# The keys' transform of a long convolution, brought into the values' form

## The chip, the cores and the metric

The kernel runs on one core of a Trainium2 chip. The metric is the device time of one execution in microseconds (us), taken over several runs; their median is compared. A profiled execution gives a span (first to last instruction) and a trace of every instruction.

## The reference

Two results of 2048 rows by 576 columns are put side by side. The first (A) is a state-space convolution: for each of 576 channels a filter K of 2048 taps is computed from 128 complex exponentials and convolved with the input u. The second (B) is linear attention with 32 heads of 18, whose features are two softmaxes.

```
A = -exp(log_A_real) + 1j * A_imag
C = (C_real + 1j * C_imag) * dt[:, None]
P = exp((A * dt[:, None])[:, :, None] * pos[None, None, :])
K = 2.0 * einsum("dn,dnl->dl", C, P).real
Kf, Uf = rfft(K, 2 * L), rfft(u_t, 2 * L)
y = irfft(Uf * Kf, 2 * L)[:, :, :L] + u * D_skip
...
phi = concatenate([softmax(p), softmax(-p)])        # of q and of k, per head
o = (phi_q @ (phi_k.T @ v)) / (phi_q @ sum(phi_k) + 1e-6)
out = concatenate([y, o @ wo])
```

The change concerns only the two transforms of A: that of the filter (in the names of the program the keys, `kd`, `kb`, `ks`) and that of the input u (here called the values, `ud`, `ub`).

## The kernel before

**Stages.** B reads 16 key tiles of 128 rows (`key_tile`) and later 16 query tiles (`query_tile`); their matrix products (`gemm`) use pairs of weights `wh`/`wl` and `vh`/`vl`. For A, 36 groups of 16 channels (`phases`, `waves`, `sizes_of`, `group`) build the filter into the tile `ks`; each nine groups complete a quarter of the channels. The transforms of length 4096 are done in two steps with the result of the first step going through DRAM:

- `u_first` (16 calls): the input's first step, 64 rows to 128 with the weights `w1`, written to `ud`.
- `k_first` with `first` (16 calls, four for each quarter): the filter's first step, 32 rows to 64 with `w1[:, 0:64]`; the eight matmuls of a call use eight tiles of TensorE's array (32 rows by 64 columns each) at once. Two stores of 64 partitions take the result to `kd`, of which there is one for each half of the channels.
- `product` (16 calls: 8 sets of frequencies `p` for each of the 2 halves): the second step of both, their product, and the first step back. Its parts are named p1 to p4. In p1 the values: 16 matmuls of 64 by 32 with the weights `ff`, on eight tiles at once, into `pu`, copied to `us`. In p2 (`times`, twice) the keys: four matmuls of 128 by 64 with the weights `fk`, a table of its own loaded twice per product, into `pk`, and a multiply by `us` on VectorE. In p3 four sums that make complex products of real ones (GpSimd or VectorE). In p4 the way back (`back`, 32 by 64), a copy and a store to `zd`.
- `last` (16 calls): the last step back, with `w3`, and the store to the output.

**Order.** Nothing is scheduled at run time. `body` only lists 2506 operations with what each reads and writes (`op`, `Plan`); the table `ORDER` at the end of the file gives the sequence in which they are emitted. In it a number is an operation, `x` takes its second engine (VectorE for ScalarE, for instance), `@` gives the PSUM banks that it takes (eight banks, 0 to 7), and `:n` puts n matmuls on zeros ahead of it, which write nothing that counts and keep TensorE occupied (line L244 of the profile, in `emit`). `Plan.run` refuses an order in which an operation stands ahead of what it needs. Each engine, and the queue SP from which all transfers are issued, works its share of the sequence strictly in that order. Buffers come from pools of fixed numbers (`tags`): a name with 2 has two buffers in turn, and who takes the third waits for the first.

Nearly all matmuls go through the helper `mm`, so they share line L302 of the profile and are told apart by the tiles they read: `kb,fk` (keys' second step), `ub,ff` (values' second step), `ks,w` (keys' first step), `ub,w` (values' first step), `ac,ff` and `cs,ff` (way back). Copies have line L307, sums L317, multiplies L321. A row such as `128*64 128x288 f32 x256` is a weight tile of 128 rows by 64 columns over 288 columns of data; TensorE executes an f32 matmul as two instructions.

## Time and profile before

| what | value |
|---|---|
| time, three runs | 551.81 us median (550.91 to 556.78) |
| profiled execution | 553.84 us, span 552.1 us |
| TensorE busy | 534.9 us (97%) |
| VectorE / ScalarE / GpSimd busy | 458.7 / 379.3 / 325.0 us |
| moved by DMA | 111.07 MB, 201 GB/s mean |
| granted TensorE clock | 0.997 mean |

Busy time of an engine is the time in which at least one of its instructions runs. Matmuls are pipelined, so a group's mean duration is longer than the distance at which they follow each other, and the groups' busy times add up to more than the engine's. "Idle before" is the time in which the engine stood still just ahead of an instruction, with what ended it.

### The profile page before, as it was taken

The numbers are of one execution on the slowest core, as the hardware profiler recorded it, in microseconds if no ns is written. First come the engines' busy times: TensorE is split into PE (matmuls) and PEld (weight loads), VectorE is DVE, ScalarE is ACT, GpSimd is POOL, SyncE is SP. The second block draws the span as 40 slices with busy tenths as digits, with TensorE's granted clock in tenths as the row PEclk, the third lists the DMA queues.
The fourth block names the chain that finished last, engine by engine and source line by source line (L and its number), as shares of the span: only waits on it lengthen the run. The fifth ranks groups of instructions, "written<-read, shape, count | busy, mean of one in ns | idle before, by whom it ended". The sixth has DMA issues, their size and how long they took to land.

```text
span 552.1 us, 18539 instructions
## 1 busy us (share of the span) xinstructions
PE 534.9 (97%) x7812; PEld 442.8 (80%) x7812; DVE 458.7 (83%) x757; ACT 379.3 (69%) x547; POOL 325.0 (59%) x473
## 2 busy tenths in 40 slices
PE   8999799999999999999999999999999999999997
PEld 7999799899978887988887766878976765776886
DVE  7999999989777999999999999998885776767541
ACT  4788857997569999897799868968873244213422
POOL 1365856787499887974599848988144245234300
PEclk9999999999999999999999999999999999999999
DMA  8964130332746778248673798675876888898976
GB/s 224 337 201 136 68 135 26 97 98 84 247 105 191 230 247 268 75 147 244 227 239 113 215 265 263 207 245 179 271 241 153 225 267 250 285 281 266 295 245 158
DMA packets 90368, 111.07 MB, mean 201 GB/s; under 512 B 5938, under 2 KB 74546, under 8 KB 90286
## 3 DMA queue, kind: packets, MB, share of 16 engines
q1 hardware_dynamic: 90286, 109.90, 65.2%
q8 instruction: 61, 1.00, 0.8%
q14 instruction: 21, 0.17, 0.1%
HBM read 65.34 MB, written 44.54 MB: 199 GB/s over the span
## 4 chain that ended last, share of the span: by engine, by line
PE 70%; DVE 11%; DMA 8%; ACT 6%; issue 3%; SPq 0%; POOL 0%; ACTq 0%; DVEq 0%
PE psum L302 64%; PE psum L557 3%; DMA ff<-in_ff_dram 2%; DMA x<-xd 1%; PE psum L244 1%; PE psum L585 1%; DMA dram<-zo 1%; DMA out_dram<-ot 1%; DMA zo<-in_xT_dram 1%; DVE small L450 1%; DMA dram<-zi 1%; DMA pa<-in_par_dram 1%; DVE x L317 1%; DVE small L441 1%; DVE e L317 1%
## 5 line engine op out<-in xcount | busy, mean ns | idle before, releaser
L302 PE MATMUL psum<-wh,x 128*128 128x288 f32 x576 | 126.0, 305 | 5.1 <-DVE x L317 3.2
L302 PE MATMUL psum<-vh,x 128*128 128x288 f32 x576 | 123.6, 301 | 0.9 <-DVE zo L307 0.8
L765 POOL TENSOR_TENSOR cs<-cs,pi 128x128 int32<-128x128 int32 (+4 forms) x180 | 105.8, 592 | 8.2
L302 PEld LDWEIGHTS psum<-wh,x 128*128 128x128 f32 x576 | 95.2, 190 | 12.5 <-issue 4.6
L302 PEld LDWEIGHTS psum<-vh,x 128*128 128x128 f32 x576 | 94.2, 188 | 7.0 <-issue 3.1
L302 PE MATMUL psum<-wl,x 128*128 128x288 f32 x320 | 94.4, 297 | 0.0
L302 PE MATMUL psum<-vl,x 128*128 128x288 f32 x320 | 93.7, 295 | 0.0
L317 POOL TENSOR_TENSOR e<-e,small 128x576 f32<-128x576 f32 (+1 forms) x28 | 46.9, 1675 | 32.0 <-DVE small L321 21.9
L819 ACT ACTIVATE psum<-psum 128x512 f32<-128x512 f32 x108 | 58.8, 583 | 9.2 <-PE psum L302 8.5
L302 PEld LDWEIGHTS psum<-wl,x 128*128 128x128 f32 x320 | 60.8, 190 | 0.0
L302 PEld LDWEIGHTS psum<-vl,x 128*128 128x128 f32 x320 | 60.2, 188 | 0.0
L823 DVE TENSOR_TENSOR cs<-psum,cs 128x1024 f32<-128x1024 f32 x36 | 43.8, 1215 | 4.5 <-ACT psum L819 4.0
L317 POOL TENSOR_TENSOR x<-zo,x 64x128 fp32r<-64x128 f32 (+1 forms) x34 | 29.7, 873 | 29.8 <-ACT x L401 28.3
L824 DVE TENSOR_TENSOR cs<-psum,cs 128x1024 f32<-128x1024 f32 x36 | 43.7, 1213 | 2.0 <-ACT psum L819 1.8
L448 ACT ACTIVATE e<-e 128x1152 f32<-128x1152 f32 x32 | 37.3, 1166 | 11.0 <-POOL e L317 6.2
L317 POOL TENSOR_TENSOR ac<-ac 128x288 f32<-128x288 f32 x36 | 29.0, 825 | 26.7 <-DVE ac L321 22.1
L453 POOL TENSOR_TENSOR o<-e 128x576 f32<-128x576 f32 x16 | 21.1, 1319 | 38.6 <-ACT e L448 37.8
L302 PEld LDWEIGHTS psum<-kvb,fT 126*128 126x128 f32 (+1 forms) x320 | 38.5, 188 | 5.6 <-issue 2.9
L302 PE MATMUL psum<-kvb,fT 126*128 126x133 f32 (+1 forms) x320 | 41.5, 279 | 0.0
L302 PEld LDWEIGHTS psum<-cs 128*32 128x32 f32 x2304 | 34.0, 110 | 8.4 <-issue 3.3
L307 ACT ACTIVATE zi<-psum 128x576 f32<-128x576 f32 x40 | 25.0, 648 | 21.4 <-PE psum L302 14.9
L302 PE MATMUL psum<-cs 128*32 128x64 f32 x2304 | 39.5, 220 | 0.0
(154 smaller groups left out, 1161.2 us busy)
## 6 DMA issues: line engine op xcount, KB each, us to landing
dram<-zi SPq DMA_DIRECT2D x16, 576.0 KB
dram<-zi SPq DMA_DIRECT2D x32, 288.0 KB
kb<-dram SPq DMA_DIRECT2D x32, 288.0 KB
ub<-dram SPq DMA_DIRECT2D x32, 288.0 KB
dram<-zo SPq DMA_DIRECT2D x32, 288.0 KB
zo<-in_xT_dram SPq DMA_DIRECT2D x24, 320.0 KB
zi<-dram SPq DMA_DIRECT2D x12, 576.0 KB
ub<-in_u_dram SPq DMA_DIRECT2D x16, 288.0 KB
```

Source lines behind the costliest of these rows:

```text
L244: self.matmul(t[0:cols, 0:n], self.zero.t[0:rows, 0:cols], self.data.t[0:rows].bitcast(BF16)[:, 0:n], start=not o[13], stop=not o[13], ski ...
L302: pe.matmul(o, l, r, start=start, stop=stop, skip_group_check=skip)
L307: op(("act", "dve"), (c_act(n), c_dve(n)), lambda e: act.activation(dst(), src(), AF.Copy) if e == "act" else dve.tensor_copy(dst(), src() ...
L317: op(eng, [c_dve(n[0]) if e == "dve" else c_pool(n[1]) for e in eng], lambda e: (dve if e == "dve" else pool).tensor_tensor(dst(), a(), b( ...
L441: op("dve", c_dve(D), lambda: dve.tensor_reduce(two(ends.t[:, :, 0]), v(), axis=AX.X, op=ALU.max, negate=True), r=[p], w=[ends])
L448: op("act", c_act(1152) + 40, lambda: act.activation(e.t, e.t, AF.Exp), r=[e], w=[e], table="exp")
L453: op("pool", c_pool(470), lambda: pool.tensor_tensor(pair.t, e.t[:, :, :, 0:9], e.t[:, :, :, 9:18], op=ALU.add), r=[e], w=[pair], lock=True)
L557: pe.transpose(tp.t[0:m, j - j0, :], e.t[:, sign, 7 * g:7 * g + GRP[g], :].rearrange("p h f -> p (h f)"), ident.t)
L765: op("pool", c_pool(2 * n * W), lambda n=n, j=j: pool.tensor_tensor(x()[:, :, :, n:2 * n], x()[:, :, :, 0:n], pi.t[:, j:j + 2, gs].bitcast ...
L819: op("act", c_act(512), lambda b=b: act.activation(b.t, b.t, AF.Exp), r=[b], w=[b], table="exp")
L823: op("dve", c_dve(64 * W), lambda: dve.tensor_tensor(F(), both(M.t), F(), op=ALU.mult), r=[M, cs], w=[cs])
L824: op("dve", c_dve(64 * W), lambda: dve.tensor_tensor(E.t[:, :, :, 32:64], both(up.t), cs.t[:, :, :, 0:32], op=ALU.mult), r=[up, cs], w=[E])
```

## The change

The filter's transform takes the form that the input's has.

- The first step makes 128 rows of 64, as `u_first` does, where it made 64 of 32. Since `ks` holds the filter in blocks of 32 rows, the 64 rows are summed in two halves: four matmuls of 32 by 128 with one half of the new table `kf`, and four with the other half that accumulate on them. The result goes to `kd` with one store of 128 partitions.
- The second step uses `ff`, the weights of the values, in the same 16 matmuls of 64 by 32. The function `turn` holds eight of them (one of two parts) and fills one pair of PSUM banks; a product calls it twice for the values and twice for the keys. The table `fk` and its 32 loads are gone.
- The multiply takes the values' both parts and one part of the keys; a sum then needs the results of both multiplies. All these tiles are `ac` (now three buffers) or `cs`; `us2`, `kb` and `fk` no longer have buffers of their own, and `ub` has five.
- `ORDER` is a new table throughout (2475 operations); the matmuls on zeros in it number 102 where there were 122.

```diff
-    return dict(w1=f(np.concatenate([w1, np.concatenate([f1, f1]), f2], 1)), fk=f(fk), ff=f(np.concatenate([fu, fi], 2)))
+    return dict(w1=f(np.concatenate([np.concatenate([f1, f1]), f2], 1)), kf=f(np.tile(f1.reshape(32, 256), (4, 1))), ff=f(np.concatenate([fu, fi], 2)))
...
-          2: "v1 o pi mg ff ub kb zo us2 ac zi", 3: "e fk x9 ot", 5: "cs", 7: "small"})
+          2: "v1 o pi mg ff zo zi", 3: "e x9 ot ac", 5: "cs ub", 7: "small"})
...
     def k_first(qt, ks):
         def one(j):
             o = B("zi", [128, 8, 4, DQ])
-            src = lambda m, c: ks.t[32 * m:32 * m + 32, 16 * j + 8 * c:16 * j + 8 * c + 8, :].rearrange("p b d -> p (b d)")
-            first(ks, src, HD, o, lambda m: o.t[:, :, 2 * m:2 * m + 2].rearrange("p b m d -> p m b d"), lambda p: p.rearrange("p m (b d) -> p m b d", b=8))
-            for c in range(2):
...
+            ps = [B("ps", [128, 2, HD], banks=2) for _ in range(2)]
+
+            def f():
+                for r in range(2):
+                    for m in range(4):
+                        mm(ps[m // 2].t[:, m % 2], kf.t[32 * m:32 * m + 32, r], ks.t[32 * m:32 * m + 32, 32 * r + 8 * j:32 * r + 8 * j + 8, :].rearrange(
+                            "p b d -> p (b d)"), r == 0, r == 1, True)
+            op("pe", 970, f, r=[kf, ks], w=ps, mode=(32, 128))
...
+        def bring(b, z, cols):
+            for par in range(2):
+                op("sp", c_dma(128 * 2304, 1152), lambda par=par: sp.dma_start(b[par].t, four(z, par)[:, :, cols]), r=[z], w=[b[par]])
+
+        def turn(b, part):
+            po = B("ps", [128, 2, HD], banks=2)
+
+            def f():
                 for c in range(4):
                     for r in range(2):
...
+                        mm(po.t[32 * c:32 * c + 32, r], fu()[64 * r:64 * r + 64, c, part, :], b[c % 2].t[64 * r:64 * r + 64, c // 2])
+            op("pe", 490, f, r=[ff, *b], w=[po], mode=(64, 32))
+            return po
+        bring(ub, ud, cs)
+        pl.step("p1")
+        home = "cs" if half and p % 2 else "ac"
+        us = B(home, [128, 2, 2, HD])
+        for part in range(2):
+            pu = turn(ub, part)
+            copy("any", lambda part=part: us.t[:, :, part], lambda pu=pu: pu.t, [pu], [us], D)
+        pl.step("p2")
+        bring(kb, kd[half], slice(0, HD))
+        acs = []
+        for part in range(2):
+            pk, ac = turn(kb, part), B(home, [128, 2, 2, HD])
+            tt("dve", lambda ac=ac: ac.t, lambda: us.t, lambda pk=pk: pk.t[:, :, None].to_broadcast([128, 2, 2, HD]), ALU.mult, [us, pk], [ac], 4 * HD)
+            acs.append(ac)
...
-        op("pe", 970, back, r=[ff, *acs], w=pz, mode=(32, 64))
+        op("pe", 970, back, r=[ff, *done, re], w=pz, mode=(32, 64))
...
-0 1 2 1125 4 1131 1192 3 5 1132 1135 1124 1134 34 51 35@0:26 20 27 1133 1137 1136 1138 6 36 359 1024 1139 52 28@2:23 29 53 39 1156 1140 1141 1155 40
+0 1 2 4 3 5 1132 1136 1135 1124 1186 1133 34 1134 51 20 1137 35@0:26 36 39 52 21@2:10 22 37 53 1138 1139 1148 1140 1155 1141 1142 1143 1105 38 27 1144
```

In the order of the instructions a row gives line, instruction, the tile written and those read, the shape, and how many follow each other. Line L302 of before is L288 of the change. On TensorE the first product that is emitted (half 0) stood so before:

```order
L302 MATMUL psum<-vl,x_4031 128x288
L302 MATMUL psum<-cs 32x64 x32
L302 MATMUL psum<-ub,ff 32x288 x16
L302 MATMUL psum<-kb,fk 64x288 x8
L302 MATMUL psum<-sel,mg 128x512 x4
```

and stands so with the change, where `ub,ff` is written for the values and for the keys alike:

```order
L571 MATMUL psum<-ident,o 128x128 x4
L572 MATMUL psum<-ident,o 128x128
L288 MATMUL psum<-ub,ff 32x288 x8
L288 MATMUL psum<-cs 32x64 x32
L288 MATMUL psum<-ub,ff 32x288 x24
L288 MATMUL psum<-sel,mg 128x512 x2
```

The values' 16 matmuls are two calls of eight, with a group's matmuls (`cs`) between them, and the keys' 16 follow the second call at once; the 8 of `kb,fk` are gone.

Later, on TensorE, a product of the second half (number 11, counted from 0) stood so before, with the way back of another product (`cs,ff`) and query tiles (`kvb,fT` and `ident,e`) between its values and its keys:

```order
L557 MATMUL psum<-ident,e 126x128 x4
L302 MATMUL psum<-ub,ff 32x288 x16
L302 MATMUL psum<-kvb,fT 128x133 x2
L302 MATMUL psum<-kvb,fT 128x76 x2
L557 MATMUL psum<-ident,e 126x128 x4
L302 MATMUL psum<-cs,ff 64x288 x16
L302 MATMUL psum<-kb,fk 64x288 x8
```

and the same product now:

```order
L543 MATMUL psum<-ident,e 72x128 x2
L288 MATMUL psum<-ub,ff 32x288 x32
L288 MATMUL psum<-kvb,fT 128x133 x6
L288 MATMUL psum<-vh,x_6832 128x288
L288 MATMUL psum<-vl,x_6832 128x288
```

All four calls follow each other in one tiling, each into a pair of banks (in the table pairs 0, 4, 6 and again 0), and query tiles' products come behind them.

On SP's queue the loads of the first products stood so before (`zi` to DRAM is the store of a first step):

```order
L634 DMA dram<-zi 128x1152 x3
L923 DMA kb<-dram 128x2x288 x2
L898 DMA ub<-dram 128x2x288
L891 DMA ff<-in_ff_dram 128x512
L898 DMA ub<-dram 128x2x288
L921 DMA fk<-in_fk_dram 128x256 x2
```

and now:

```order
L656 DMA mg<-gd 64x768
L608 DMA dram<-zi 128x1152
L886 DMA ub<-dram 128x2x288
L877 DMA ff<-in_ff_dram 128x512
L886 DMA ub<-dram 128x2x288 x3
```

The loads of `fk` are no longer in the queue; those of the keys have the line and the name of the values' loads.

266 lines of the change are left out of this document (108 added, 158 removed).

## The prediction

> **What bounds the kernel now.** I read the page first: engines, slices, the chain of waits by engine.
>
> ```profile
> span 552.1 us, 18539 instructions
> PE 534.9 (97%) x7812; PEld 442.8 (80%) x7812; DVE 458.7 (83%) x757; ACT 379.3 (69%) x547; POOL 325.0 (59%) x473
> ...
> PE 70%; DVE 11%; DMA 8%; ACT 6%; issue 3%; SPq 0%; POOL 0%; ACTq 0%; DVEq 0%
> ```
>
> TensorE is busy for 97% of the span and carries 70% of the chain that ended last. 552.1 - 534.9 = 17.2 us are all that it stood idle. The share is an average, so next come four stretches (busy us of each engine, granted clock, DMA share, GB/s).
>
> ```profile
> 0.00:110.00 110.00, 104.94 (x1446) 96.78 (x1447) 102.46 (x161) 82.14 (x112) 60.57 (x105) 0.98 0.50 153
> 110.00:265.00 155.00, 152.59 (x2566) 132.37 (x2568) 137.33 (x242) 128.14 (x184) 116.24 (x167) 1.00 0.57 175
> 265.00:400.00 135.00, 135.00 (x2165) 104.37 (x2155) 124.33 (x196) 113.89 (x163) 100.33 (x154) 1.00 0.72 224
> 400.00:552.10 152.10, 142.33 (x1655) 109.26 (x1653) 94.57 (x161) 55.14 (x92) 47.81 (x48) 1.00 0.82 242
> ```
>
> From 110 to 400 us TensorE lacks 2.4 us of 290: work added to or taken from it there moves the end one for one. Ahead of 110 us VectorE is nearly as full. Behind 400 us TensorE idles for 152.1 - 142.3 = 9.8 us while the DMA engines are busy for 0.82 of the time: there the transfers share in the bound.
>
> What the change touches on TensorE are four groups of the view of groups by line and form (busy us, mean ns of one execution; an f32 matmul is executed twice, so 128 matmuls read x256).
>
> ```profile
> L302 PE MATMUL psum<-kb,fk 128*64 128x288 f32 x256 | 35.7, 414 | 1.4 <-DVE ac L936 0.8 <-DVE cs L321 0.4 <-DVE fT L307 0.2
> L302 PE MATMUL psum<-ub,w 64*128 64x288 f32 x128 | 20.8, 424 | 0.1
> L302 PE MATMUL psum<-ub,ff 64*32 64x288 f32 x512 | 19.5, 408 | 2.1 <-DMA ff<-in_ff_dram 2.1
> L302 PE MATMUL psum<-ks,w 32*64 32x288 f32 x256 | 13.2, 426 | 1.3 <-issue 1.3
> ```
>
> `kb,fk` is the keys' second transform, `ub,ff` the values' second one, `ks,w` the keys' first one, `ub,w` the values' first one. Busy time here is the time in which at least one matmul of the group runs, so these sums can be compared across tilings.
>
> **The keys' second transform.** Removed: 16 products times 8 matmuls of 128 rows by 64 columns, 35.7 us. Added: 16 times 16 matmuls of 64 by 32 over the same 288 columns with the same `ff` weights, which is what `ub,ff` is: 19.5 us. Change: -16.2 us. The other end: if each of the 32 new calls stood alone between other tilings, it would cost what a lone call of eight tiles costs, 0.67 us from 421.08 to 421.75 in the timeline below, 32 x 0.67 = 21.4, and the change -14.3. I take -16.2, since the new order mostly puts such calls side by side.
>
> **The keys' first transform.** Removed: 16 calls of 8 matmuls of 32 by 64, all eight tiles at once, 13.2 us. Added: 16 calls of 8 matmuls of 32 by 128, four tiles at once, two deep (the second accumulates on the first). The trace has no 32 by 128 form. Its nearest row is `ub,w`, 64 by 128, two tiles at once and two deep, 16 calls as well: 20.8 us, +7.6. Bounds: 13.2 us (nothing added) below. Above, the call has sixteen weight loads against eight in `ub,w`; could only two run at a time, a call would take twice as long, 41.6 us, +28.4. The rows of the loads speak against that end: in `ks,w` the sixteen loads of a call span 0.23 us, although four row groups are addressed.
>
> ```profile
> 28.54 1.24 PE L302 MATMUL psum<-ub,w 64*128 64x288 f32 x8
> 29.71 0.40 PE L302 MATMUL psum<-vh,x 128*128 128x288 f32 x1
> ...
> 421.08 0.74 PE L302 MATMUL psum<-ks,w 32*64 32x288 f32 x16
> 421.75 0.40 PE L302 MATMUL psum<-wh,x 128*128 128x288 f32 x1
> ...
> 421.08 0.23 PEld L302 LDWEIGHTS psum<-ks,w 32*64 32x64 f32 x16 [0.17 <-issue]
> ...
> 434.73 2.16 PE L302 MATMUL psum<-kb,fk 128*64 128x288 f32 x16 [0.16 <-DVE fT L307]
> 436.82 0.38 PE L302 MATMUL psum<-kvb,fT 126*128 126x133 f32 x1
> ```
>
> **Sum, made twice.** From the groups: -16.2 + 7.6 = -8.6 us. From single visits (start of a call to start of what follows): call one pass of all tiles that work at once a round. `kb,fk` has 16 executions on 2 tiles, 8 rounds in 2.09 us; `ks,w` 16 on 8, 2 rounds in 0.67. So a round is 1.42 / 6 = 0.237 us and a visit adds 0.20. `ub,w`, 8 on 2, should then take 4 x 0.237 + 0.20 = 1.15; it took 1.17. Rounds before: 128 + 32 + 64 (`ub,ff`) = 224. Rounds after: 64 + 64 + 64 = 192. 32 x 0.237 = 7.6 us less. Counted over the two orders, TensorE changes its tiling 240 times before and 228 times after, which at 0.20 is 2.4 us less: -10.0 in all. I take -8.6, since the groups cover all calls and not three.
>
> The page TensorEngine Tiling of the Trainium skill (Key Properties) says that a change of tiling drains TensorE; the 0.20 us of a visit agree with it. By that rule the 12 changes saved are real and the sum is -10.0; without it they are nothing and the rounds alone give -7.6.
>
> **Loads and stores.** Dropped: 32 loads of `fk` and 32 issues on SP's queue; one `kf` load comes early.
>
> ```profile
> q1 hardware_dynamic: 90286, 109.90, 65.2%
> ...
> dram<-zi SPq DMA_DIRECT2D x32, 288.0 KB
> ...
> fk<-in_fk_dram SPq DMA_DIRECT2D x32, 128.0 KB
> ...
> L921 SPq DMA_DIRECT2D fk<-in_fk_dram x32: 333/458/1183, 275.8 to 495.3; - x32
> ```
>
> 32 x 128 KB = 4.2 MB of 109.9 MB, so about 4.2 / 109.9 x 65.2% x 552 = 14 us of all DMA engines, half of it behind 400 us. SP issues them in 32 x 0.46 = 15 us, in line with the `ub`, `kb` and `zo` transfers. On the path I count 0: TensorE waited for transfers of a product only 2.1 us (`ff`, above). At best these 2.1 us go. The first transform's 32 stores become 16 of double size; the last of each half may land later by one old store, and covered it is by other products and query tiles; uncovered I bound it at 1.5 us a half.
>
> **The rest of a product.** Two copies and two multiplies of the same sizes stay, and four sums of 288 (over all products 45 of 64 on GpSimd instead of 49). One wait is new: a sum needs both multiplies instead of one.
>
> ```profile
> POOL ac L317 <- DVE ac L321: 22.1, 6, 7.1
> ```
>
> GpSimd already waits 22.1 us for these multiplies. The first sum of a product can wait one multiply longer, 1.35 us (row under the banks, below); behind it on GpSimd stand the angle steps of the kernel's groups and the query tiles' sums, which ScalarE and VectorE wait for, and TensorE's last step of the product waits for the sums. From 265 to 400 us GpSimd is idle for 34.7 of 135, so I count 0; uncovered it is at most 16 x 1.35 = 21.6 us, an end that would need GpSimd on the path, where the chain has it at 0%.
>
> The matmuls that only keep TensorE occupied (L244) go from 122 to 102. They stand where the old order expected a wait, so I count 0; at best 20 x 10.8 / 71 = 3 us.
>
> ```profile
> L244 PE MATMUL psum<-ident,zero 128*128 128x256 bf16 x71 | 10.8, 320 | 1.5 <-DVE zero L340 1.5
> ```
>
> **The new order as a whole.** Its waits can't be read from a trace of the old one. I take the 17.2 us of idle as they are. One of them shows how far they can move:
>
> ```profile
> 64.77 0.29 PE L302 MATMUL psum<-wl,x 128*128 128x288 f32 x1
> 68.23 0.61 PE L302 MATMUL psum<-wh,x 128*128 128x288 f32 x1 [3.17 <-DVE x L317]
> ...
> 68.00:71.50 3.50, 3.27 (x14) 3.27 (x15) 3.50 (x6) 2.87 (x4) 1.76 (x3) 0.54 0.49 157
> ```
>
> A wait of 3.17 us was followed by 3.5 us at a granted clock of 0.54, which loses 3.5 x 0.46 = 1.6 more: 4.8 us in one place that the change doesn't touch. A new order can lose it or have a second one. TensorE: Matmul & The Clock Gate of the Trainium skill (Part 1) puts the threshold at an idle window of about 3.4 us; this trace agrees in kind: behind 110 us, where no wait is named that is as long, the clock stands at 1.00.
>
> **Result of the sum.** The profiled execution took 553.84 us, 1.7 more than its span; 553.8 - 8.6 = 545.2. It stands 2.0 above the median of the three runs, 551.8; on that footing the forecast is 543.2, 1.6% less.
>
> **Rivals.**
> *The tail gives nothing (no change).* Eight of the sixteen products run behind 400 us. If transfers set the pace there, their share of 16.2, 8.1 us, turns into waits, and 552.1 - 0.5 = 551.6 is left (551.3 as median). For it: DMA share 0.82, 9.8 us idle. Against: 2.1 MB fewer are moved there too, about 7 us of the DMA engines' time, so both resources shrink alike. Chance 0.25.
>
> *Banks (slower).* The new calls come in runs of up to four, each into a pair of the eight PSUM banks. A run is 8 rounds, 1.9 + 0.2 us. The pairs come free only after two copies and two multiplies:
>
> ```profile
> L307 DVE COPY us<-psum 128x576 f32<-128x576 f32 x12 | 8.8, 748 | 1.9 <-PE psum L302 1.8
> L321 DVE TENSOR_TENSOR ac<-us,psum 128x1152 f32<-128x1152 f32 x24 | 31.6, 1351 | 3.7 <-PE psum L302 3.0 <-ACT zo L307 0.2
> ```
>
> 0.75 + 2 x 1.35 = 3.45 us of VectorE's time stays as it is, and TensorE, through sooner by 1.0 us a product, meets the same full banks. If it then waits 1.0 us each time, the 16.2 us are lost, the +7.6 stay: 559.7 (559.4 as median). It is slower by over 1% once the loss exceeds 8.6 + 5.5 = 14.1, or 0.88 us a product. For it: VectorE is 92% busy from 265 to 400. Against: kb's matmuls waited 1.4 us in all, and the order puts other tiles behind a run. TensorEngine Tiling (PSUM Bottleneck) in the Trainium skill says that tiling speeds up TensorE but not the emptying of PSUM; this is that rule, and the 1.4 us show no sign of it yet. Chance 0.10.
>
> *More than the sum (faster).* The wait at 64.8 us goes too: 543.2 - 4.8 = 538.4. Nothing in the change aims there. Chance 0.15.
>
> The forecast keeps 0.50.
>
> **How the numbers follow.** 1% is about what can be told from no change: 546.3 and 557.3. Of the forecast's 0.50 about 0.05 lie above 546.3 (uncovered stores, 3 us, with the lower sum). Faster: 0.45 + 0.15 = 0.60; same: 0.05 + 0.25 = 0.30; slower: 0.10. The range leaves out the banks and some of the lowest case: from 538.4 less half of the 3 us of filler, 537, to 551.3 plus the run-to-run 1, 553. The likeliest case alone is 540 to 547.
>
> **What would show it.** `ub,ff` with x1024 at some 39 us and no `kb,fk`; the 32 by 128 form near 21 us; TensorE busy near 526; idle near 17. Wrong if the new form costs far more than 1.3 us a call, if TensorE's idle behind 400 us grows by the 8 us that its work shrank, or if waits on the multiplies (L307 in the new numbering) follow the runs of four.

## The result

The changed kernel took 548.55 us (median of 20 runs, 546.16 to 552.82); the kernel before took 551.75 in the same series (20 runs). The ratio is 0.9935, with a 95% interval of 0.991 to 0.996: 0.65% faster, 3.2 us. By the prediction's bound of 1% that is no change. The forecast of 543.2 was 5.4 us too low; the range 537 to 553 holds the time.

The page of the changed kernel (the profiled execution took 552.82 us, the longest of its runs; a second profile follows under e10): span, engines, the queue of the transfers, and the chain of waits by engine.

```profile
span 551.0 us, 18919 instructions
PE 529.0 (96%) x8048; PEld 440.9 (80%) x8048; DVE 455.8 (83%) x762; ACT 378.6 (69%) x549; POOL 319.0 (58%) x463
...
q1 hardware_dynamic: 85566, 105.80, 61.6%
...
PE 34%; DVE 3%; ACT 3%; DMA 2%; issue 1%; SPq 1%; POOL 0%; ACTq 0%; POOLq 0%
```

TensorE is busy for 5.9 us less, and idle for 551.0 - 529.0 = 22.0 us where it was idle for 17.2. (The chain of this profile could be followed for less than half of the span, so its shares say little.) The groups of TensorE's matmuls that the change touches:

```profile
L288 PE MATMUL psum<-ub,ff 64*32 64x288 f32 x1024 | 40.1, 418 | 2.5 <-ACT zo L293 0.9 <-ACT ac L293 0.6 <-ACT ks L293 0.5
L288 PE MATMUL psum<-ub,w 64*128 64x288 f32 x128 | 21.4, 426 | 0.0
L288 PE MATMUL psum<-ks,kf 32*128 32x288 f32 x256 | 20.4, 424 | 0.0
```

Both second transforms together cost 40.1 us where they cost 35.7 + 19.5 = 55.2, so -15.1; the keys' first one costs 20.4 where it cost 13.2, so +7.2. That is -7.9 of TensorE's work, close to the forecast's -8.6. (TensorE's busy time fell by 5.9 only: other rows grew, `sel,mg` from 24.7 to 27.2 and `cs` from 39.5 to 41.3 us, partly where the clock was low.) The work went; the time did not go with it. The same four stretches as before:

```profile
0.00:110.00 110.00, 106.92 (x1522) 98.04 (x1523) 100.60 (x167) 80.71 (x111) 68.60 (x109) 1.00 0.51 159
110.00:265.00 155.00, 150.68 (x2416) 131.34 (x2414) 135.72 (x237) 127.67 (x183) 107.38 (x159) 1.00 0.55 177
265.00:400.00 135.00, 126.31 (x2375) 94.36 (x2375) 123.82 (x187) 113.55 (x162) 101.90 (x155) 0.96 0.60 185
400.00:551.00 151.00, 145.10 (x1756) 117.19 (x1745) 95.69 (x174) 56.64 (x95) 41.10 (x40) 1.00 0.80 246
```

From 265 to 400 us TensorE was never idle before. Now it is idle for 8.7 us of 135, and its granted clock there is 0.96. One wait of that idle time has no releaser:

```profile
368.88 0.22 PE L288 MATMUL psum<-cs 128*32 128x64 f32 x1 [2.41 <-issue]
```

Ahead of 110 us TensorE is busy for 2.0 us more, behind 400 us it idles for 5.9 us where it idled for 9.8. So the question is the stretch in the middle: TensorE was 100% busy in it, work was taken away, and idle time came in its place.

For the experiments one stretch of it is marked by two events that every kernel has: the start of the 61st execution of `sel,mg` (the first step of a group, `g0`) and the start of the last execution of `cs` (a group's sum, `g4`). It is called the marked stretch. Its row in the view of stretches, for the kernel before:

```profile
265.21:412.87 147.66, 147.66 (x2436) 114.55 (x2430) 135.66 (x212) 123.69 (x177) 105.89 (x159) 1.00 0.73 226
```

TensorE 100%, VectorE 92%, ScalarE 84%, GpSimd 72% busy.

Each kernel has one profile, of one execution, so these stretches have a spread of their own. The part ahead of the marked stretch moves most: of the twelve profiles in the old order seven have a wait of 3.2 us near 65 us, five have one of 0.9 us or less there. What the runs gain or lose against the kernel before is taken from the ratio.

### The profile page after: what moved, and what is told of

It is laid out like the page before. It is cut to its first block, busy times and chain, and to the rows that moved or that the text cites. A ratio compares the mean times of both kernels' runs of the same rounds, so it can differ in the third digit from the quotient of the medians.

```text
span 551.0 us, 18919 instructions
## 1 busy us (share of the span) xinstructions
PE 529.0 (96%) x8048; PEld 440.9 (80%) x8048; DVE 455.8 (83%) x762; ACT 378.6 (69%) x549; POOL 319.0 (58%) x463
## 3 DMA queue, kind: packets, MB, share of 16 engines
q1 hardware_dynamic: 85566, 105.80, 61.6%
## 5 line engine op out<-in xcount | busy, mean ns | idle before, releaser
L288 PE MATMUL psum<-wh,x 128*128 128x288 f32 x576 | 123.3, 300 | 1.7 <-DMA x<-xd 0.9
L288 PE MATMUL psum<-vh,x 128*128 128x288 f32 x576 | 123.7, 302 | 1.2 <-DVE v L293 0.6
L739 POOL TENSOR_TENSOR cs<-cs,pi 128x64 int32<-128x64 int32 (+4 forms) x180 | 106.1, 596 | 9.2
L288 PEld LDWEIGHTS psum<-vh,x 128*128 128x128 f32 x576 | 94.9, 190 | 7.4 <-issue 2.9
L288 PEld LDWEIGHTS psum<-wh,x 128*128 128x128 f32 x576 | 94.2, 188 | 7.7 <-issue 2.6
L288 PE MATMUL psum<-vl,x 128*128 128x288 f32 x320 | 94.3, 297 | 0.5 <-DVE vl L376 0.5
L288 PE MATMUL psum<-wl,x 128*128 128x288 f32 x320 | 93.9, 296 | 0.1
L288 PEld LDWEIGHTS psum<-vl,x 128*128 128x128 f32 x320 | 60.9, 190 | 0.9 <-DVE vl L376 0.9
L288 PEld LDWEIGHTS psum<-wl,x 128*128 128x128 f32 x320 | 60.2, 188 | 0.3 <-DVE wl L360 0.3
L303 POOL TENSOR_TENSOR x<-zo,x 128x512 fp32r<-128x512 f32 (+1 forms) x34 | 31.6, 934 | 45.1 <-ACT x L387 31.6
L303 POOL TENSOR_TENSOR e<-e,small 128x1152 f32<-128x1152 f32 (+1 forms) x26 | 43.8, 1684 | 12.7 <-DVE small L307 5.6
L288 PE MATMUL psum<-cs 128*32 128x64 f32 x2304 | 41.3, 223 | 4.5 <-issue 4.3
L303 POOL TENSOR_TENSOR e<-small,e 128x576 f32<-128x576 f32 x22 | 25.7, 1170 | 32.5 <-DVE small L431 30.0
L288 PEld LDWEIGHTS psum<-cs 128*32 128x32 f32 x2304 | 35.0, 111 | 11.7 <-issue 7.7
L288 PE MATMUL psum<-ub,ff 64*32 64x288 f32 x1024 | 40.1, 418 | 2.5 <-ACT zo L293 0.9
L288 PEld LDWEIGHTS psum<-kvb,fT 126*128 126x128 f32 (+1 forms) x320 | 38.8, 190 | 4.6 <-issue 1.7
L293 ACT ACTIVATE zi<-psum 128x576 f32<-128x576 f32 x43 | 26.5, 651 | 23.2 <-PE psum L288 17.4
L288 PE MATMUL psum<-kvb,fT 126*128 126x133 f32 (+1 forms) x320 | 41.2, 278 | 0.1
```

The source lines that it names most:

```text
L288: pe.matmul(o, l, r, start=start, stop=stop, skip_group_check=skip)
L293: op(("act", "dve"), (c_act(n), c_dve(n)), lambda e: act.activation(dst(), src(), AF.Copy) if e == "act" else dve.tensor_copy(dst(), src() ...
L303: op(eng, [c_dve(n[0]) if e == "dve" else c_pool(n[1]) for e in eng], lambda e: (dve if e == "dve" else pool).tensor_tensor(dst(), a(), b( ...
L739: op("pool", c_pool(2 * n * W), lambda n=n, j=j: pool.tensor_tensor(x()[:, :, :, n:2 * n], x()[:, :, :, 0:n], pi.t[:, j:j + 2, gs].bitcast ...
```

## The form and the order taken apart

**e1, the new form in the old order.** Both transforms as in the change, but the sequence of the operations and their banks as before (nine operations come later than there, because of buffers). The table's first row:

```diff
-0 1 2 4 3 5 1132 1136 1135 1124 1186 1133 34 1134 51 20 1137 35@0:26 36 39 52 21@2:10 22 37 53 1138 1139 1148 1140 1155 1141 1142 1143 1105 38 27 1144
+0 1 2 1125 4 1132 1193 3 5 1133 1136 1124 1135 34 51 35@0:26 20 27 1134 1138 1137 1139 6 36 359 1024 1126 1140 52 28@2:23 29 53 39 1157 1141 1142 1156
...
```

> The new form (keys through the values' tables) in the old order of the list: each operation stands where its counterpart stood, the values' second step as two calls side by side, fk loads and the second store of a first step dropped, 9 operations moved back to where their inputs are there. Theory 'list': the new form is worth 8.6 us of TensorE one for one, and the new list gives some 5 of them away in waits of its own; the old list should then give about 543 to 545 us (ratio 0.985). Theory 'other engines': between 265 and 400 us VectorE and the PSUM banks stop TensorE as soon as its work shrinks, whatever the list; then about 547 to 551 (0.993 to 1.0).

Measured: 551.84 us, ratio 1.0038 (1.0003 to 1.0073). The new form alone gains nothing. The work is nearly as small as in the change (`ub,ff` 41.7 us, `ks,kf` 20.2 us), yet the marked stretch is as long as before:

```profile
268.43:416.08 147.65, 144.65 (x2563) 111.67 (x2558) 135.78 (x212) 123.83 (x177) 106.01 (x159) 1.00 0.66 208
```

TensorE lost 3.0 us of busy time in it and stands idle for 3.0. The next two runs take the two steps apart.

**e5, the first step alone** (old order):

```diff
+            ps = [B("ps", [128, 2, HD], banks=2) for _ in range(2)]
...
+                        mm(ps[m // 2].t[:, m % 2], w1.t[32 * m:32 * m + 32, 128 * r:128 * r + 128], ks.t[32 * m:32 * m + 32, 32 * r + 8 * j:32 * r + 8 * j + 8, :].rearrange(
+                            "p b d -> p (b d)"), r == 0, r == 1, True)
+            op("pe", 970, f, r=[w1, ks], w=ps, mode=(32, 128))
```

> The kernel before with its old order, the keys' first transform alone in the new form (32 to 128, two deep; four tiles at once), the second as it was; a call takes its weights from the table of the other transforms, so that no buffer is added, and the output is that of another matrix: only the work counts. TensorE's work grows by 7.2 us (20.4 for 13.2). Theory 1 of the prediction (one for one): 551.6 + 7 = 559. Theory 2 (what is added to a TensorE that is full always costs; what is taken away between 265 and 413 us gives nothing): also 557 to 559, since an addition counts. If the first transform's cost is hidden (rival): 552.

Measured: 559.77 us, ratio 1.0143 (1.0097 to 1.0189), +7.9 us. The step's group grew from 13.2 to 21.0 us, +7.8. Over the whole run what is added to TensorE counts one for one, as the forecast had it. In the marked stretch, which holds a quarter of these calls (1.9 us), the stretch grew by 1.95 us and TensorE stayed without a gap:

```profile
270.89:420.50 149.61, 149.61 (x2437) 116.55 (x2430) 135.30 (x212) 123.81 (x177) 105.88 (x159) 1.00 0.71 222
```

Outside it the one profile doesn't follow the work as closely: ahead of the stretch, with half of the calls, it is 5.7 us longer, and behind it, with the last quarter, 1.1 us shorter (138.1 for 139.2). One for one is shown in the marked stretch and for the whole, not for each part.

**e6, the second step alone** (old order, nine operations later than there):

```diff
-            op("pe", 970, f, r=[kf, ks], w=ps, mode=(32, 128))
...
+            src = lambda m, c: ks.t[32 * m:32 * m + 32, 16 * j + 8 * c:16 * j + 8 * c + 8, :].rearrange("p b d -> p (b d)")
+            first(ks, src, HD, o, lambda m: o.t[:, :, 2 * m:2 * m + 2].rearrange("p b m d -> p m b d"), lambda p: p.rearrange("p m (b d) -> p m b d", b=8))
```

> The kernel with the keys' second transform alone in the values' form, the first in its old form, in the old order (nine steps later than there because of buffers). The two halves don't fit, so the output is not the reference's; every operation is run. TensorE's work falls by 15 to 16 us, half of it between 265 and 413 us, half behind. Theory 1 (one for one): 536. Theory 2 (removals before 413 us give nothing, those behind count): 543 to 546, and the time from the first step of the 27th to the last product's half before 413 us is as in the kernel before. Rival (the tail gives nothing too): 551.

Measured: 549.77 us, ratio 0.9962 (0.993 to 0.9995), -2.1 us. The work fell by 13.3 us (`ub,ff` 41.9 us for 55.2). Theory 1 asked for 536. The marked stretch, and the chain of waits by engine:

```profile
270.99:417.58 146.59, 142.84 (x2564) 110.14 (x2558) 135.44 (x212) 123.78 (x177) 106.25 (x159) 1.00 0.68 209
```

```profile
PE 57%; DVE 18%; DMA 11%; ACT 8%; issue 4%; POOL 1%; SPq 1%; DVEq 0%; ACTq 0%; POOLq 0%
```

TensorE's busy time in the stretch fell by 4.8 us, the stretch by 1.1; 3.75 us of idle came up. TensorE's share of the chain fell from 70% to 57%, VectorE's rose from 11% to 18%, that of the transfers from 8% to 11%. Behind the stretch (412.87 to 552.1 before, 417.58 to 550.9 here) 5.9 us were gained, of about 6.7 that half of the products lost there. Measured against e3 below, which has TensorE's work of before in this part and took 137.0 us for it, the gain is 3.7. So the stretch in the middle keeps most of its removed work, and the end gives more than half of it back. The parts don't add up to the 2.1 us of the median: this profile is the longest of the run's executions (552.69 us), and it lost 5.8 us ahead of the stretch, where nothing was changed in the work. What the ahead part costs in the other executions was not seen.

## What holds the marked stretch

All these runs are of the kernel before, in its old order and old forms, with work left out on one engine or several.

**e3, VectorE lightened.** Half of the groups' in-place multiply is left out:

```diff
-        op("dve", c_dve(64 * W), lambda: dve.tensor_tensor(F(), both(M.t), F(), op=ALU.mult), r=[M, cs], w=[cs])
+        op("dve", c_dve(64 * W), lambda: dve.tensor_tensor(F()[:, 0], M.t, F()[:, 0], op=ALU.mult), r=[M, cs], w=[cs])
```

> The kernel before with the same half of VectorE's in-place multiply left out. TensorE has no idle between 265 and 400 us there. Both theories: under 2 us off ahead of any effect at the start of the kernel (0 to 110 us, where VectorE is nearly full); if it gains as much as the changed kernel, VectorE was a bound of the old kernel too, and the difference between the two kernels isn't VectorE.

Measured: 547.24 us, ratio 0.9932 (0.9899 to 0.9964), -3.8 us. VectorE has 6.5 us less in the marked stretch, which became no shorter but 1.5 us longer:

```profile
260.31:409.51 149.20, 148.12 (x2435) 114.62 (x2430) 129.12 (x213) 123.69 (x177) 105.83 (x159) 1.00 0.72 223
```

The gain stands ahead of it, in a start 4.9 us earlier: the wait of 3.17 us near 65 us, which the prediction quoted, is 0.5 us here and no half clock follows (the last section returns to it). Behind the stretch, with nothing left out, the profile is 2.2 us shorter than before's. Differences between single profiles of 1.5 us in the marked stretch, and of some 2 us behind it, therefore prove nothing by themselves.

**e4, TensorE lightened.** Half of the products' way back (`ac,ff` and `cs,ff`) is left out:

```diff
-            for part in range(2):
+            for part in range(1):
...
-                        mm(pz[c % 2].t[64 * r:64 * r + 64, c // 2], fi()[32 * c:32 * c + 32, r, part, :], acs[r].t[32 * c:32 * c + 32, 2 * part], part == 0, part == 1, True)
+                        mm(pz[c % 2].t[64 * r:64 * r + 64, c // 2], fi()[32 * c:32 * c + 32, r, part, :], acs[r].t[32 * c:32 * c + 32, 2 * part], True, True, True)
```

> The kernel before, with only one of the two parts of each product's way back multiplied (16 x 8 matmuls left out, so the result of the convolution is not the reference's): about half of the 20.9 us of the groups ac,ff and cs,ff, 10 us, goes from TensorE between 299 and 511 us; nothing else changes. It asks how much of TensorE's work counts under the old list. Theory 'list': 8 to 10 us off (TensorE sets the pace). Theory 'other engines': 3 to 5 us off, with new idle of TensorE between 265 and 400 us.

Measured: 546.42 us, ratio 0.9906 (0.9869 to 0.9942), -5.2 of the 8.5 us by which the two groups shrank (20.9 to 12.4). The marked stretch holds half of these calls; counted from start to start they lost 3.3 us in it. It is 0.8 us shorter, and 1.4 us of idle came up:

```profile
261.91:408.78 146.87, 145.46 (x2308) 111.58 (x2302) 135.48 (x212) 123.86 (x177) 105.76 (x159) 1.00 0.73 227
```

Lightening TensorE alone, or VectorE alone, does not shorten the stretch as its work shrinks, then. Both together may, or more. Unlike e1 and e6, these runs keep the old order and its buffers unaltered.

**e7, both edits at once.**

```diff
+        op("dve", c_dve(64 * W), lambda: dve.tensor_tensor(F()[:, 0], M.t, F()[:, 0], op=ALU.mult), r=[M, cs], w=[cs])
...
+            for part in range(1):
```

> The kernel before, old order and old forms, with both lightenings at once that were tried apart: half of the products' way back left out on TensorE (10 us, half of it between 265 and 413 us), and half of the in-place multiply of the groups left out on VectorE (7 us between 265 and 400). Apart they gave 4.3 and 5.1 us, none of it between the 61st size step (265 us) and the last size sum (413 us), a stretch of 147.6 us. Theory 2 (there TensorE and VectorE are both full, so that one alone can't shorten it): the stretch falls to 143 to 144 us, the time to 538. Theory 3 (the stretch is paced by the written order's chained waits, not by an engine's load): 146 to 147.5 us, time 542, the sum of the two.

Measured: 544.75 us, ratio 0.9868 (0.9825 to 0.9911), -7.3. The stretch is 146.81 us, no shorter than with TensorE's edit alone, where theory 2 asked for 143 to 144: it is out.

```profile
262.06:408.87 146.81, 145.06 (x2307) 111.64 (x2302) 129.25 (x213) 123.79 (x177) 105.78 (x159) 1.00 0.73 227
```

**e11, TensorE and ScalarE.** As e4, and half of the columns of each exponential:

```diff
-            op("act", c_act(512), lambda b=b: act.activation(b.t, b.t, AF.Exp), r=[b], w=[b], table="exp")
+            op("act", c_act(512), lambda b=b: act.activation(b.t[:, 0:8], b.t[:, 0:8], AF.Exp), r=[b], w=[b], table="exp")
```

> The kernel before with half of the products' way back left out on TensorE, as in an earlier run (546.4 us; 146.9 us from the 61st size step to the last size sum), and in addition half of ScalarE's exponentials of the groups left out (each over half of its columns, in place): 46 executions between 268 and 413 us at 0.58 us, so about 46 x 0.25 = 11 us less on ScalarE there. Theory A (ScalarE's exponentials are the second bound of the stretch, behind TensorE): the stretch shrinks by the 3.3 us that TensorE lost in it, to 144 or less; time 543. Theory B (no single engine's load is, the pace is that of the written order's chained waits): 146 or more, time 546.

Measured: 548.69 us, ratio 0.9933 (0.9903 to 0.9963), -3.7 us. The profile has the wait of 3.2 us near 65 us again, which that of e4 doesn't have, and the stretch starts 2.5 us later; whether that explains the higher time is not shown. ScalarE lost 9.4 us in the stretch, and it took 146.63, where theory A asked for 144 or less:

```profile
264.45:411.08 146.63, 144.79 (x2308) 111.57 (x2302) 135.48 (x213) 114.31 (x177) 105.78 (x159) 1.00 0.74 227
```

**e12, all four engines.** e4, e3 and e11 together, and half of the columns of the products' sums (one of the two lines):

```diff
-            tt(("pool", "dve"), lambda: ac.t[:, 0], lambda: ac.t[:, 0], lambda: ac.t[:, 3], ALU.subtract, [ac], [ac], HD)
+            tt(("pool", "dve"), lambda: ac.t[:, 0, 0:144], lambda: ac.t[:, 0, 0:144], lambda: ac.t[:, 3, 0:144], ALU.subtract, [ac], [ac], HD)
```

> The kernel before with all four engines lightened in the stretch from 265 to 413 us: half of the products' way back left out on TensorE, half of the groups' in-place multiply on VectorE, half of the exponentials on ScalarE, and half of the columns of the products' sums on GpSimd and VectorE. Theory A (engine loads, several near full at once): now nothing is left that is full, and the stretch falls from 147.6 to 143 us or less; time 538 or less. Theory B (the order's chained waits, whatever the loads): 146; time 543 to 544.

Measured: 541.27 us, ratio 0.9805 (0.9765 to 0.9844), -10.8 us.

```profile
259.52:405.20 145.68, 144.44 (x2308) 111.56 (x2302) 126.93 (x211) 113.93 (x177) 97.07 (x159) 1.00 0.74 229
```

Of the 3.3 us that TensorE lost in the stretch 0.8 arrive with its own edit, 0.9 with VectorE's added, 1.0 with ScalarE's, 2.0 with all four. The first three can't be told apart. The fourth decides between the theories less than its bounds suggest: theory A's 143 us lies below the 144.44 for which TensorE is still busy here, so it could not be reached, and B's 146 isn't met either. In e12 the chain of waits lies on TensorE for 94% of the stretch, and TensorE idles for 1.2 us. So lightening TensorE with one more engine doesn't bring the removed work back; with all four more than half may come back, if the difference is more than the spread. That the engines hand over to each other in a written order, so that one that is through sooner waits at the next hand-over, is an explanation that fits; that it and not the loads sets the pace was not shown. Two rivals were not tried: GpSimd lightened without the others, and the transfers, which the chain of waits has for at most 18 us of the stretch (e3).

## The new order

**e2, the changed kernel with VectorE lightened** (the edit of e3).

> The changed kernel with VectorE's in-place multiply in each of the 36 groups done on half of its elements only (the other half is left out, so the filter is not the reference's): 36 x about 0.55 us, 20 us less on VectorE, most of it ahead of 400 us; TensorE's work is the same. Theory 'list' (TensorE sets the pace): under 2 us off. Theory 'other engines': 5 us or more off the changed kernel's 548.5, with TensorE's idle between 265 and 400 us falling from 8.7 towards 3.

Measured: 547.01 us, ratio 0.9915 (0.9888 to 0.9943) against the kernel before, so 1.5 us under the changed kernel's 548.55 (1.1 by the ratios). VectorE alone isn't what the new order waits for either.

**e8, the changed kernel with half of the way back** (the edit of e4 in the new code).

> The changed kernel with half of the products' way back left out on TensorE (10 us of matmuls, as in the same experiment on the kernel before, which gave 5.1 us of it). One for one: 548.5 - 10 = 538.5. If the new order has the same weakness between 265 and 400 us and gives back only what lies behind it: 543 to 544. If the half clock near 378 to 393 us, which followed three short waits, comes again it is the order that makes it: TensorE then has 6 us or more of idle and slow clock there once more.

Measured: 545.45 us, ratio 0.9883 (0.9833 to 0.9933); 3.1 us under the changed kernel's 548.55, for 8.3 us of work (20.3 to 12.0); by the ratios it is 2.9 to 3.9. The new order gives back removed work no better than the old one.

**e10, the changed kernel once more**, for a second profile.

> The changed kernel unaltered, once more on this chip, for a second profile beside the one in which TensorE also stood for 2.4 us near 369 us with no releaser named. Theory: that wait was a disturbance of one execution and is gone, the three short waits near 380 us and the half clock behind them are there again; 548.5. Rival: both are there again, so both belong to the new order.

Measured: 548.42 us (545.55 to 552.08), ratio 0.9954 (0.9922 to 0.9985). This profiled execution was the shortest of its runs, 545.55 us:

```profile
span 543.8 us, 18919 instructions
```

```profile
265.44:396.00 130.56, 124.29 (x2351) 93.40 (x2344) 123.03 (x187) 113.45 (x162) 101.34 (x153) 0.97 0.61 191
```

The wait of 2.41 us near 369 us is gone: it belonged to that execution. Between the starts of the 61st `sel,mg` and the end this execution took 543.8 - 265.4 = 278.4 us, where before took 552.1 - 265.2 = 286.9 and e1 550.3 - 268.4 = 281.9. e9, below, took 549.6 - 271.5 = 278.1; the first profile of the change, with the wait of 2.41 us in it, 284.7. Behind that point TensorE's work fell by 15.1 and rose by half of 7.2, so by 11.5. In these profiles the old order turned 5.0 of them into time, the new one 8.5, with some 2 us of spread on each. It did so with a different split: 130.56 us to the last `cs` and 147.8 behind it, against 147.66 and 139.2. Ahead of the point the new order stands at 265.4 as the old one did at 265.2: the 3.6 us of the first step's other half are in it, and the stall near 65 us is gone, as it is in all five profiles of the new order.

**e9, the three waits near 380 us filled.** In the first profile of the changed kernel three short waits follow each other (order of the instructions, TensorE), and the clock falls to half behind them (stretches of 5 us; the second number from the end but one is the clock):

```profile
383.30 0.50 PE L288 MATMUL psum<-sel,mg 64*128 64x512 f32 x2 [0.20 <-DVE ac L307]
384.60 0.51 PE L288 MATMUL psum<-sel,mg 64*128 64x512 f32 x2 [0.80 <-DVE ac L307]
385.80 0.59 PE L288 MATMUL psum<-sel,mg 64*128 64x512 f32 x2 [0.69 <-ACT zo L293]
```

```profile
380.00:385.00 5.00, 4.00 (x75) 2.15 (x73) 4.27 (x7) 4.97 (x6) 0.32 (x1) 1.00 0.14 31
385.00:390.00 5.00, 4.30 (x53) 2.96 (x55) 4.55 (x6) 3.56 (x8) 0.48 (x1) 0.61 0.96 290
390.00:395.00 5.00, 5.00 (x105) 4.43 (x100) 5.00 (x7) 4.19 (x8) 3.67 (x4) 0.71 0.72 217
```

In the three stretches the columns behind GpSimd's are clock, DMA share and GB/s: 1.00, then 0.61 and 0.71. Two of the waits end with a multiply behind a keys' second step (`ac`), one with a copy of a way back (`zo`). The edit adds matmuls on zeros inside the waits:

```diff
-678 679 2065@4 2120 705@1 2068x 2019x 2122 2121 709 2066x 710 2069 2149 2148 2242 2071@2 706 2073@4 707 680 1925 2119 2123@06:1 2074 1906@45 2072 1926
-1927 1929 1930 2075 1846 2124 2125 2216 1946@23 1907@01 2218 649 1928 2127 1931 1908@45:9 2217 1935 2126 1945@67 1932 834 758 1974 1933@0 1973 1937
+678 679 2065@4 2120 705@1 2068x 2019x 2122 2121 709 2066x 710 2069 2149 2148 2242 2071@2 706 2073@4 707 680 1925 2119 2123@06:4 2074 1906@45:6 2072 1926
+1927 1929 1930 2075 1846 2124 2125 2216 1946@23:6 1907@01 2218 649 1928 2127 1931 1908@45:9 2217 1935 2126 1945@67 1932 834 758 1974 1933@0 1973 1937
```

> The changed kernel, nothing left out, its order kept; only 15 more of the matmuls that keep TensorE occupied are put at the place near 380 us where three short waits follow one another (3 more ahead of the products' way back, 6 each ahead of the first step of groups 15 and 16). They run inside the waits, at about 0.11 us each. If the order makes the slow clock there (theory): no stretch at half clock between 375 and 395 us, 3.4 us less, 545 against the changed kernel's 548.5. If the slow clock comes from something else, or the waits move on behind it (rival): 548.5.

Measured: 547.81 us (546.32 to 551.35), ratio 0.993 (0.9898 to 0.9963); e10, on the same chip in the same set, 548.42. The two longer waits there are now 0.46 us each, and the half clock is gone from the place, in the profile of e9,

```profile
380.00:385.00 5.00, 4.83 (x86) 3.35 (x86) 4.34 (x7) 4.51 (x5) 1.96 (x3) 1.00 0.06 7
385.00:390.00 5.00, 3.73 (x67) 2.65 (x70) 4.51 (x6) 4.88 (x11) 0.80 (x1) 1.00 0.81 244
```

while e10, left as it was, has it again:

```profile
380.00:385.00 5.00, 4.25 (x45) 2.90 (x47) 4.47 (x5) 3.36 (x8) 0.40 (x1) 0.55 0.95 287
385.00:390.00 5.00, 5.00 (x124) 4.42 (x118) 4.93 (x7) 4.19 (x9) 3.50 (x4) 0.77 0.69 207
```

The profiles of e2 and e8, which have these waits unfilled, have it there too. So the order does make the slow clock there, as far as four profiles without the filling and one with it show. But it does not cost the 3.4 us that were expected: the marked stretch with the waits filled took 130.13 us, without 130.56, and the times differ by 0.6 us, within their spread.

```profile
271.52:401.65 130.13, 122.70 (x2366) 92.52 (x2359) 122.33 (x185) 113.41 (x162) 101.36 (x153) 1.00 0.62 191
```

A TensorE at half clock for 6.8 us there costs next to nothing; that others are later than it in this stretch would explain it. e9 is the lowest median of the kernels that leave nothing out, and not distinguishable from the change itself.

## Were it the multiplies that free the banks?

The third rival named VectorE's multiplies behind the keys' second step. In e6's marked stretch they do end the largest part of TensorE's named waits (1.8 of 3.3 us). Two runs, e14 and e15, take half of them away; e13 is the base of the first.

**e13** is e6 with half of the way back left out (the edit of e4), so that the other half of the multiplies has no reader:

```diff
-            for part in range(2):
+            for part in range(1):
...
+                        mm(pz[c % 2].t[64 * r:64 * r + 64, c // 2], fi()[32 * c:32 * c + 32, r, part, :], re.t[32 * c:32 * c + 32, r, part], True, True, True)
```

> The kernel with the keys' second transform alone in the new form (old order), and in addition half of the products' way back left out on TensorE (10 us, as in the earlier runs on before and after). It is the base for the next run. The half way back gave 5.1 us on the kernel before and 3.1 on the changed one: 549.8 - 3 to 5 = 545 to 547; the stretch between the 61st size step and the last size sum stays at 146 to 146.6 us.

Measured: 544.35 us, ratio 0.9858 (0.9808 to 0.9908).

**e14** leaves that half of the multiplies out as well:

```diff
-            tt("dve", lambda ac=ac: ac.t, lambda: us.t, lambda pk=pk: pk.t[:, :, None].to_broadcast([128, 2, 2, HD]), ALU.mult, [us, pk], [ac], 4 * HD)
+            tt("dve", lambda ac=ac, part=part: ac.t[:, :, part], lambda part=part: us.t[:, :, part], lambda pk=pk: pk.t, ALU.mult, [us, pk], [ac], 4 * HD)
```

> As the run before it, and in addition half of each of the products' 32 multiplies left out on VectorE (the half that the shortened way back doesn't read; 0.65 us less each, 21 us in all, 10 of it between 265 and 413 us), so that the PSUM pairs behind the keys' second transform come free sooner. Banks (the third rival's mechanism): the stretch falls from some 146 us by most of the 9 us of TensorE's work that is gone there, to 140 or less, and the waits on the multiplies go; time under 541. Order (chained waits of many kinds): 145 or more, time 1 to 2 us under the run before it.

Measured: 545.47 us, ratio 0.9865 (0.9826 to 0.9904). The marked stretches of e13 and of e14, in this order:

```profile
261.64:407.32 145.68, 140.00 (x2435) 107.06 (x2430) 134.90 (x212) 123.52 (x177) 106.06 (x159) 1.00 0.67 210
```

```profile
265.76:411.29 145.53, 140.83 (x2436) 108.44 (x2430) 126.92 (x212) 123.73 (x177) 105.50 (x159) 0.99 0.67 211
```

The longest of TensorE's named waits in it, of e13 (what waited, releaser, total us, times, longest),

```profile
PE psum L293 <- DVE ac L312: 2.1, 4, 0.9
PE psum L293 <- DVE zo L298: 0.7, 1, 0.7
```

and of e14:

```profile
PE psum L293 <- DVE zo L298: 1.6, 1, 1.6
PE psum L293 <- DVE cs L817: 0.5, 1, 0.5
PE psum L293 <- issue: 0.4, 1, 0.4
PE psum L293 <- POOL ac L308: 0.3, 1, 0.3
```

The waits on the multiplies (L312) are gone, 8 us of VectorE's work with them, and the stretch is as long as it was: a wait on a copy (`zo`) took their place, and the clock fell behind it (0.99 over the stretch, about 1.5 us). Where the forecast's mechanism of the banks asked for 140 us or less, 145.5 came. The multiplies are where the waits show in this stretch, not what sets its length. In e14 GpSimd takes their place in the chain of waits: it has 24% of the stretch there and 4% in e13.

**e15, the same pair of edits on the kernel before** (the second sum of a product then reads the half that is still written):

```diff
-            tt("dve", lambda: ac.t.rearrange("p (x y) n -> p x y n", x=2), lambda: u_at(r)[:, None].to_broadcast([128, 2, 2, HD]),
-               lambda: pk.t[:, :, None].to_broadcast([128, 2, 2, HD]), ALU.mult, [us[r], pk], [ac], 4 * HD, with_=home)
+            tt("dve", lambda: ac.t[:, 0:4:3], lambda: u_at(r), lambda: pk.t, ALU.mult, [us[r], pk], [ac], 4 * HD, with_=home)
```

> The kernel before with half of the way back and half of the products' multiplies left out in the same way. Without the second the kernel took 546.4 and the stretch 146.9 us. Banks: the stretch falls by the 3.3 us of work that the half way back took from TensorE there, to 144. Order: 146 or more.

Measured: 545.91 us, ratio 0.9875 (0.9831 to 0.9918); without the second edit (e4) it was 546.42. The marked stretch is 147.01 us, against 146.87 in e4, where the banks asked for 144:

```profile
265.71:412.72 147.01, 144.87 (x2308) 111.43 (x2302) 127.53 (x212) 123.95 (x177) 105.38 (x159) 1.00 0.73 227
```

Behind it e15 took 131.6 us where e4 took 134.0, so the multiplies may count at the end of the old kernel; e13 and e14 don't show it (132.3 and 132.6, the latter at a clock of 0.97).

## Why the prediction was wrong, step by step

- **The sizes were right.** Keys' second step: forecast -16.2, measured -15.1. Keys' first step: forecast 20.8 for the form that the trace did not show, measured 20.4. Sum: -8.6 forecast, -7.9 measured. In the old order the second step gave less, -13.3 (e6), which is beyond the forecast's other end of -14.3. The rounds alone gave -7.6 and rounds with changes of tiling -10.0. What the 12 changes saved are worth was not tried apart. By the rule of TensorEngine Tiling (Key Properties) in the Trainium skill, that a change of tiling drains TensorE, they would be worth something; the -7.9 doesn't show it.
- **Loads, stores, the rest of the product, fillers: counted as 0, not tested.** The transfers' share fell from 65.2% to 61.6%, and no run ties the time to it; what they gave was not tried apart. The matmuls on zeros took as long as before (17.5 and 17.3 us over all their forms).
- **The step that failed: "from 110 to 400 us TensorE lacks 2.4 of 290 us: work added to or taken from it there moves the end one for one."** It holds for work added (e5: +7.9 us of time for +7.8 of work). It fails for work removed: over the whole run e6 gave -2.1 us of 13.3, e4 -5.2 of 8.5, e8 -3.1 of 8.3. Within the marked stretch the removals give almost nothing (e1 0.0, e4 0.8, e6 1.1 us, all within the spread of single profiles), and idle time takes the place of most of them. A busy share of 100% shows only that nothing else is later than TensorE; how much earlier the others are it doesn't show. VectorE stood at 92% in the same rows, and the chain's share of other engines rose as soon as TensorE had less to do. Perfetto Trace Analysis in the Trainium skill (Identifying the Most-Contended Engine) holds that matmul busy time is a poor measure of how near TensorE is to its peak and asks, among others, for the busy share of the weight loads. Read so, TensorE had some 22% to spare in the marked stretch (weight loads 114.55 of 147.66 us, an estimate). e6 agrees with that warning, e5 does not: an addition had no room at all in that stretch.
- **The stretch behind it was read the wrong way round.** The forecast made the tail ("gives nothing") its likeliest rival. The tail gives more than half of its share back (e6 3.7 to 5.9 of about 6.7 us); the middle doesn't. The rival's mechanism is seen in part: in e6 TensorE waits 3.2 us behind the marked stretch for loads of `ub`, which it did not do before. The sign that the forecast named, idle growing behind 400 us, did not come in the changed kernel (5.9 us for 9.8). The measured time, 548.55, lies between the forecast's 543.2 and the rival's 551.3, and that the range held it is luck: no mechanism of the forecast led there.
- **Banks.** The waits on the multiplies that were to show it came, 2.1 us in e13 and 1.8 in the first profile of the changed kernel (TensorE's waits between 268 and 415 us), but e14 and e15 reject them as what sets the marked stretch of the old order. In the new order it was not tried.

```profile
PE psum L288 <- DVE ac L307: 1.8, 4, 0.8
```

- **Idle kept at 17.2 us.** It became 22.0. The gain of the last rival did come, since the stall near 65 us is in none of the new order's profiles, and the time still didn't fall to that rival's 538.4.
- **The order.** Counted as neutral; in fact the form in the old order gains nothing (e1), so all of the measured 0.65% needs the new one.

What stays open: what sets the marked stretch once TensorE has less to do there, a chain of hand-overs in the written order, several engines nearly full at once, or GpSimd or the transfers, which were not relieved apart. Four engines relieved in part bring back 2.0 of 3.3 us there. An order written anew for lighter work would be one test, and wasn't made.

## What to carry to other kernels

An engine that is 100% busy tells the price of work added to it, not the gain of work removed; before counting a removal, look how full the next engines are in the same stretch, and leave out half of some work on the full engine to see what comes back. Here the order of instructions was written out beforehand, and removed work turned into many short waits of different names; removing the cause that the longest of them named (e14) only changed the name. Form and order should be measured apart, and one profile of each kernel is too few where single executions differ by more than the effect.

## What the runs showed of the hardware

**Half clock after short waits.** No wait of the changed kernel near 380 us is longer than 0.80 us, yet three of them within 2.7 us (0.20, 0.80, 0.69) were followed by a clock of 0.61 and 0.71 over 10 us, and so again in e10 (0.20, 0.80, 0.76; clock 0.55, 0.77). With matmuls on zeros in the gaps, and 0.46 us left of each of the longer two, the clock stayed at 1.00 (e9). TensorE: Matmul & The Clock Gate of the Trainium skill (Part 1) ties the slow clock to an idle window of about 3.4 us; here a window that was idle only in part was enough.

**VectorE held while GpSimd works.** Up to this place the kernel before and e4 issue the same instructions. In the profile of before VectorE's sum of 192 columns takes 2.23 us,

```profile
62.90 2.23 DVE L321 TENSOR_TENSOR ax<-ax,ay 128x192 f32<-128x192 f32 x1
65.17 1.45 DVE L704 TENSOR_SCALAR ax<-ax 128x192 f32<-128x192 f32 x1
66.54 1.64 DVE L317 TENSOR_TENSOR x<-zo,x 128x512 fp32r<-128x512 f32 x1
```

beside a long sum of GpSimd:

```profile
62.60 2.32 POOL L317 TENSOR_TENSOR e<-e,small 128x1152 f32<-128x1152 f32 x1
```

In e4 it starts 0.5 us earlier, ahead of GpSimd's, and takes 0.55 us; the next one is held instead:

```profile
62.36 0.55 DVE L321 TENSOR_TENSOR ax<-ax,ay 128x192 f32<-128x192 f32 x1
62.94 2.14 DVE L704 TENSOR_SCALAR ax<-ax 128x192 f32<-128x192 f32 x1
65.00 0.84 DVE L317 TENSOR_TENSOR x<-zo,x 128x512 fp32r<-128x512 f32 x1
```

```profile
62.65 2.31 POOL L317 TENSOR_TENSOR e<-e,small 128x1152 f32<-128x1152 f32 x1
```

In both the instruction that began inside GpSimd's ended with it (65.1 beside 64.9 us). In the kernel before the two behind it are slow as well (1.45 and 1.64 us, the last 0.84 in e4), beside GpSimd's next instructions. `x` is ready at 68.2 us there and at 65.8 in e4, and TensorE waits 3.17 us with half clock behind, or 0.92 us without. The loss of 0.5 us ahead of it thus goes with some 4 us behind. That GpSimd holds VectorE is read from the ends that coincide, no run moved the one to see the other move. The runs of the kernel before spread over 8.4 us (549.36 to 557.76), and that is why the stretches above are compared beside the times. GPSIMD Engine Reference of the Trainium skill (Specifications) says that GpSimd's interfaces to the on-chip memory are shared with VectorE, with contention for VectorE's instructions that have two inputs there or run in a mode with two ports; the two-input sum agrees, and L704, with one input, was held as well (no row shows its mode).
